# Routed attention and SoLU block: the exponentials' buffers as parts of one tile, with ScalarE's waits on itself declared away

## The chip, the cores and the metric

The kernel runs on one core of one Trainium2 chip. The time is device microseconds of one execution, from the core's first to its last work with the start and end around it; lower is better. Engines are named as in the profile: PE is TensorE (PEld its weight loads), ACT is ScalarE, DVE is VectorE, POOL is GpSimd, SP is SyncE, which here issues most DMAs. A q behind an engine (ACTq, SPq) means its sequencer, the part that waits for semaphores and issues.

## The reference

Two parts follow one another. The attention part takes q, k and v of 4 batches, 8 heads, 768 positions, 64 columns. Each query and key is assigned to the nearest of 16 normalised centroids of its head, and a query attends only to keys of its own cluster:

```python
mask = q_assign[:, :, :, None] == k_assign[:, :, None, :]
scores = scale * np.matmul(q, k.transpose(0, 1, 3, 2))
scores = np.where(mask, scores, -1000000000.0)
attn = np.exp(scores - max) ; attn = attn / (sum + 1e-09)
out = np.matmul(attn, v)
```

The heads are then laid side by side (3072 tokens of 512), and the second part computes

```python
h = x @ w_in                       # 512 -> 1024
sm = softmax(h) ; solu = h * sm
ln = (solu - mean) / sqrt(var + 1e-06) * g_ln
out = ln @ w_out                   # 1024 -> 512
```

## The kernel before

**Attention.** q and k of a pair of heads are loaded by SP into `raw` (four loads of 32 partitions for each tile, `load`, L400), turned by DVE into `xt` (L408), and cast by POOL into `qk`, whose rows below the 64 columns carry one-hot cluster rows, so that one matmul gives the score with the mask in it. `scores` (L602) fills one PSUM bank `sps` of 128 keys by up to 512 query columns; there are three such banks in rotation and 294 bank fillings in all. `expo` (L608) turns each bank into a bf16 tile `e` on ACT. There are nine `e` buffers in rotation. `values` (L625) uses 128-column pieces of `e` as matmul weights against v with a column of ones, so that numerator and denominator come out together in `ops`; `normalise` (L637, L650, DVE) divides.

**Second part.** For each of 24 blocks of 128 tokens: x is transposed (`xT`, by a DMA at L680), multiplied by w_in into two of three PSUM banks of `hreg` (`f_h`, L711), its negated maximum is taken on DVE (`f_max`, L717), ACT takes the exponential with its row sum (`f_exp`, L723, tiles `e_sb` and `esum`), DVE multiplies (`f_u`, L730), a DMA transposes `u` (L735), PE multiplies by w_out (`f_y`, L775), DVE takes the variance, POOL the factor alpha (L751 to L760, it reads `esum`), ACT or DVE scales (`f_scale`, L790, L792), and a DMA stores. The very last block is stored in two halves, and one of these halves borrows a buffer of `e_sb` as fp32.

**Order.** The two parts run interleaved. The order on each engine is written out by hand in the tables of the class `Weave`; each instruction then waits on semaphores for what it needs. Each engine counts its finished instructions in one semaphore (here named after the engine: PE, Activation and so on), and a wait is for a count.

**Buffers and waits.** Before the change, `e`, `e_sb` and `esum` are taken from pools in rotation: each use is a new tile in an old place. The framework then orders the new write behind everything that touched the old place: behind the matmuls that read it (a wait on PE) and behind the earlier write on ACT itself (a wait on Activation). An instruction of ACT holds one wait; where there are two, the program has an instruction EVENT_SEMAPHORE ahead of it that holds the other. So 275 of the 294 exponentials of L608 stand behind an EVENT_SEMAPHORE. In these the EVENT_SEMAPHORE holds the wait on PE (the later of the bank being full and the old buffer being read), and the exponential itself holds the wait on Activation. In the program the first of these waits on Activation is for count 9, ahead of the thirteenth activation of the queue that counts: the write nine exponentials back.

Of the kernel before, what the change touches and what calls it, by code (L numbers as in the profile page):

```python
# [10 lines left out]
F32 = mybir.dt.float32  # L11
BF16 = mybir.dt.bfloat16
# [3 lines left out]
Act = mybir.ActivationFunctionType  # L16
# [153 lines left out]
def kernel(  # L170
# [11 lines left out]
    nc = tc.nc  # L182
# [3 lines left out]
    P = 128  # L186
# [7 lines left out]
    d_ff = moe_w_in.shape[1]  # L194
    n_dc = d_model // P
    n_fc = d_ff // P
    FF2 = 512
    n_ff2 = d_ff // FF2
# [4 lines left out]
    exp_scale = BIAS_C / (D ** 0.5)  # L203

    const = ctx.enter_context(tc.tile_pool(name="const", bufs=1))
    big = ctx.enter_context(tc.tile_pool(name="big", bufs=1))
# [2 lines left out]
    xtp = ctx.enter_context(tc.tile_pool(name="xtp", bufs=6))  # L209
    pr = ctx.enter_context(tc.tile_pool(name="pr", bufs=3))  # L210
    vp = ctx.enter_context(tc.tile_pool(name="vp", bufs=3))
    ep = ctx.enter_context(tc.tile_pool(name="ep", bufs=9))
    mo = ctx.enter_context(tc.tile_pool(name="mo", bufs=2))
    sm = ctx.enter_context(tc.tile_pool(name="sm", bufs=4))
    ps_s = ctx.enter_context(tc.tile_pool(name="ps_s", bufs=3, space=bass.MemoryType.PSUM))
    ps_h = ctx.enter_context(tc.tile_pool(name="ps_h", bufs=1, space=bass.MemoryType.PSUM))
# [15 lines left out]
    def uses(ins, *banks, keep=90):  # L232

        for other, theirs in bank_uses[-keep:]:
            if other.ins.engine == ins.ins.engine:
                continue
            if not set(banks) & set(theirs):
                tc.declare_no_dep(ins.ins, other.ins, reason="other banks of the region")
            else:
                tc.add_manual_dep(ins.ins, other.ins.name, SYNC, reason="same bank of the region")  # L240
        bank_uses.append((ins, banks))
# [40 lines left out]
    for b in range(B):  # L282
        for p in range(n_pair):
            a, c = 2 * p, 2 * p + 1
# [38 lines left out]
    def wide(n, j):  # L323
        return sum(w for _, _, _, w, _ in UNITS[n]["banks"][j])
# [31 lines left out]
    def apart(b, p):  # L356


        return by_token(b) and not halves_of(b, p)
# [231 lines left out]


    es, sps_, opss, xs = {}, {}, {}, {}

    def scores(n, k):
        u = UNITS[n]
        b = u["b"]
        sps_[n, k] = ps_s.tile([P, 512], F32, name="sps", tag="sps")
        for h, kt, s0, w, c0 in u["banks"][k]:
            r = used(b, h)  # L600
            keys = slice(kt * P, (kt + 1) * P) if by_token(b) else slice(kt, S, n_t)
            nc.tensor.matmul(sps_[n, k][:, c0:c0 + w], side(b, h // 2, 1, h % 2, keys)[r],  # L602
                             side(b, h // 2, 0, h % 2, slice(s0 * P, s0 * P + w))[r])

    def expo(n, k):
        w = wide(n, k)
        es[n, k] = ep.tile([P, 512], BF16, name="e")
        nc.scalar.activation(es[n, k][:, :w], sps_[n, k][:, :w], Act.Exp, scale=exp_scale,  # L608
                             bias=-exp_scale)

    def place_of(n, j):

# [40 lines left out]
    xTs, ff = {}, {}  # L653
    n_f = B * n_t
# [6 lines left out]
    def pair_of(f):  # L661
        return hreg[:, 0:2, :] if f % 2 == 0 else hreg[:, 1:3, :]

    def both(f):
        return (0, 1) if f % 2 == 0 else (1, 2)
# [52 lines left out]
                                     negate=True), *both(f))  # L718

    def f_exp(f):  # L720
        ff[f, "esum"] = sm.tile([P, 1], F32, name="esum")
        ff[f, "e"] = mo.tile([P, n_ff2, FF2], BF16, name="e_sb")
        uses(nc.scalar.activation(ff[f, "e"][:], pair_of(f), Act.Exp, bias=ff[f, "nmax"][:],  # L723
                                  accum_out=ff[f, "esum"][:]), *both(f))

    def f_u(f, half=None):
        if not half:
# [20 lines left out]
    def f_eps(f):  # L748

        ff[f, "es1"] = sm.tile([P, 1], F32, name="es1")  # L750
        nc.gpsimd.tensor_scalar(ff[f, "es1"][:], ff[f, "esum"][:], scalar1=1e-3, scalar2=None,  # L751
                                op0=Alu.mult)

    def f_alpha(f):
# [25 lines left out]
    def f_scale(f, e, half=None):  # L780

        if half:
            y = mo.tile([P, n_ff2, FF2], BF16, name="e_sb")[:].rearrange(
                "p a f -> p (a f)").bitcast(F32)
        else:
            y = mo.tile([P, d_model], F32, name="y")[:]
        n = d_model if half is None else d_model // 2
        ff[f, "o", half], src = y[:, :n], (ff[f, "y"] if half is None else hreg[:, half, :n])
        if e == "ACT":
            ins = nc.scalar.activation(y[:, :n], src, Act.Copy, scale=ff[f, "alpha"][:])  # L790
        else:
            ins = nc.vector.tensor_scalar(y[:, :n], src, scalar1=ff[f, "alpha"][:], scalar2=None,  # L792
                                          op0=Alu.mult)
        if f == n_f - 1:
            uses(ins, half)
# [40 lines left out]
    for hh in range(2):  # L836
        for x in range(2):
# [19 lines left out]
                            scalar1=c_inv[:], scalar2=None, op0=Alu.mult)  # L857
# [43 lines left out]
    for idx, (b, p) in enumerate(pairs):  # L901
        first = first_of(b, p)
        if by_token(b):
            for hf, i in ((hf, i) for hf in range(2) for i in range(2)):
# [9 lines left out]
                e = "ACT" if (b, p) == (0, 0) and i == hf else "DVE"  # L914
# [5 lines left out]
        for i in range(2):  # L920
# [31 lines left out]
            for hh in range(2):  # L952
                for hf in range(2) if halves_of(b, p) else (None,):
# [3 lines left out]
                    e = "ACT" if hf is not None and i == 1 else "POOL"  # L957
# [18 lines left out]
    for idx, (b, p) in enumerate(pairs):  # L976
        first = first_of(b, p)
        for hf in range(2) if halves_of(b, p) else (None,):
# [23 lines left out]
            for j, (i, part) in enumerate(hots):  # L1002
                e = ("DVE", "POOL")[j % 2] if half else "POOL" if apart(b, p) else "SP"
# [9 lines left out]
                    (lambda e, b=b, p=p, hf=hf: blank(b, p, hf, e)),  # L1013
                    [f"pl{t}.1.{part}" for part in range(2)], also={"DVE": 0.2})

    ring_s, ring_e = 3, 9
    for i, (n, k) in enumerate(BANKS):
        u = UNITS[n]
        b = u["b"]
        p = u["subs"][0][0] // 2  # L1020
        t0 = time_of[n, k]
        nd = set()
        for h, kt, s0, w, _ in u["banks"][k]:
            p, hh = h // 2, h % 2
# [17 lines left out]
        if i >= ring_e:  # L1042
            n0, k0 = BANKS[i - ring_e]
            nd += [f"V{n0}.{j}" for j, (h, su) in enumerate(UNITS[n0]["subs"])
                   if any(spots[n0, h, su, kt][0] == k0 for kt in range(n_t))]
        add(f"E{n}.{k}", "ACT", 0.05 + wide(n, k) / 1200, t0 - 1,
            (lambda e, n=n, k=k: expo(n, k)), nd, ["E{}.{}".format(*BANKS[i - 1])] if i else [])
    prev = None
    for g, ns in enumerate(GROUPS):
# [50 lines left out]
    for f in range(n_f):  # L1100
# [15 lines left out]
        for f2 in range(n_ff2):  # L1116
            for part in range(2):
# [16 lines left out]
        nd = ([f"hm{f}"] + ([f"u{f - 2}"] if f >= 2 else []) +  # L1134
              ([f"at{f - 4}"] if f >= 4 else []))
        add(f"ex{f}", "ACT", 1.09, s + 1, (lambda e, f=f: f_exp(f)), nd)
        nd = [f"ex{f}"]
        if f >= 3:
# [16 lines left out]
        for f2 in range(n_ff2):  # L1155
# [3 lines left out]
        add(f"ag{f}", "DVE", 0.13, s + 8, (lambda e, f=f: f_aggr(f)),  # L1159
            [f"bn{f}.0", f"bn{f}.1"] + reader("al", f))  # L1160
        add(f"at{f}", "POOL", 0.22, s + 6, (lambda e, f=f: f_eps(f)), [f"ex{f}"] + reader("al", f))
        add(f"al{f}", "POOL", 1.0, s + 8, (lambda e, f=f: f_alpha(f)),
            [f"ag{f}", f"at{f}"] + reader("sc", f))
# [16 lines left out]
        if f == n_f - 1:  # L1180
            add(f"sc{f}.0", "DVE", 0.45, s + 5, (lambda e, f=f: f_scale(f, e, 0)),
                [f"y{f}.1", f"al{f}", f"ou{f - 2}"], also={"ACT": 0.36})
            add(f"ou{f}", "SP", 0.54, s + 8, (lambda e, f=f: f_out(f, 0)), [f"sc{f}.0"],
                move=0.8)
            add(f"sc{f}.1", "ACT", 0.36, s + 5, (lambda e, f=f: f_scale(f, e, 1)),
                [f"y{f}.3", f"al{f}", f"u{f}.1"], also={"DVE": 0.45})
            add(f"oz{f}", "ACT", 0.5, s + 8, (lambda e, f=f: f_out(f, 1, nc.scalar)),
                [f"sc{f}.1"])
        else:
            add(f"sc{f}", "ACT", 0.6, s + 5, (lambda e, f=f: f_scale(f, e)), nd,  # L1190
                give=None if f == n_f - 3 else "m", also={"DVE": 0.69})
            add(f"ou{f}", "SP", 0.54, s + 8, (lambda e, f=f: f_out(f)), [f"sc{f}"], move=0.8)
# [68 lines left out]
```

## Time and profile before

| | |
|---|---|
| median of three runs | 224.8 us (224.51 to 225.04) |
| span of the profiled execution | 223.1 us |
| what the median has beyond that span | 1.7 us |
| PE busy | 214.7 us, 96% of the span |
| ACT busy | 192.1 us, 86% |
| DVE busy | 197.0 us, 88% |
| exponentials of L608 | 294 instructions, 151.1 us |
| EVENT_SEMAPHORE of ACT at L608 | 275 instructions, 17 ns each |

The profile lists no whole time of the profiled execution other than its span; the span leaves out start and end. Busy time of PE is modelled and its matmuls overlap, so 96% does not mean that PE is at its peak. EVENT_SEMAPHORE is not counted as busy time. "Idle before, releaser" is the time that an engine stood still just ahead of a group of instructions, and what ended it. The chain is the work that ended last, followed back from the end.

### The profile page before, as it was taken

How to read it: one execution, taken by the hardware profiler on the slowest of the kernel's cores; microseconds unless marked ns; L12 is line 12 of the kernel's file. 1: busy time of each engine (PE TensorE's matmuls, PEld its weight loads, DVE VectorE, ACT ScalarE, POOL GpSimd, SP SyncE). 2: the span in 40 equal slices, each digit the busy share in tenths (PEclk: the TensorE clock that was granted, in tenths of full speed). 3: DMA queues.
4: the chain of work that ended last, by engine and by line, in shares of the span. 5: the costliest groups of instructions: out<-in, count | busy, mean ns of one | idle time of the engine just before them, and what ended most of it. 6: DMA issues, size and time to landing. Idle time of an engine off the chain costs nothing.

```text
span 223.1 us, 6642 instructions
## 1 busy us (share of the span) xinstructions
PE 214.7 (96%) x2422; PEld 149.8 (67%) x2454; DVE 197.0 (88%) x359; ACT 192.1 (86%) x372; POOL 127.0 (57%) x247
## 2 busy tenths in 40 slices
PE   7899999999999999999999999999999999999994
PEld 6576656677566777776577667787677777755452
DVE  3799898999999989999998999887999889888982
ACT  3779999999888999998889899999999998983363
POOL 3499842774793999547668543944796403022331
PEclk9999999999999999999999999999999999999999
DMA  6999888989999998899999879199940528385923
GB/s 151 333 299 183 240 171 240 341 203 200 166 180 180 207 156 152 190 174 205 149 268 152 175 147 240 67 207 220 223 59 9 98 51 140 79 156 148 177 80 141
DMA packets 125679, 38.80 MB, mean 174 GB/s; under 512 B 115016, under 2 KB 121168, under 8 KB 125648
## 3 DMA queue, kind: packets, MB, share of 16 engines
q1 hardware_dynamic: 123904, 37.87, 82.3%
q10 hardware_dynamic: 1744, 0.52, 1.0%
q8 instruction: 19, 0.31, 0.6%
q14 instruction: 12, 0.10, 0.1%
HBM read 23.11 MB, written 6.29 MB: 132 GB/s over the span
## 4 chain that ended last, share of the span: by engine, by line
PE 83%; ACT 5%; DVE 4%; issue 3%; DMA 3%; SPq 1%; ACTq 0%; DVEq 0%
PE sps L602 27%; PE hreg L711 17%; PE yps L775 17%; PE ops L625 14%; ACT e L608 5%; PE csc L451 4%; DMA raw<-in_q_dram 2%; PE hreg L387 1%; DVE u L730 1%; DMA raw<-in_k_dram 1%; PE hreg L575 1%; PE hreg L775 1%; PE csc L446 1%; DVE bs L741 1%; DVE xt L408 0%
## 5 line engine op out<-in xcount | busy, mean ns | idle before, releaser
L608 ACT ACTIVATE e<-sps 128x512 bf16<-128x512 f32 (+1 forms) x294 | 151.1, 599 | 12.2 <-PE sps L602 10.2
L602 PE MATMUL sps<-qk 80*128 80x256 bf16 (+5 forms) x636 | 94.0, 264 | 1.4 <-ACT e L608 0.5
L602 PEld LDWEIGHTS <-qk 80*128 80x128 bf16 (+1 forms) x636 | 60.1, 121 | 27.6 <-issue 9.0
L625 PEld LDWEIGHTS <-e 128*128 128x128 bf16 x1152 | 50.4, 97 | 12.4 <-issue 1.9
L625 PE MATMUL ops<-v,e 128*128 128x65 bf16 x1152 | 55.0, 193 | 0.1
L711 PE MATMUL hreg<-w_in_sb,xT 128*128 128x512 bf16 x173 | 49.1, 379 | 1.3 <-DVE u L730 0.2
L775 PE MATMUL yps<-w_out_c,uT 128*128 128x512 bf16 x171 | 46.5, 379 | 0.6
L515 POOL COPY qk<-oht 32x384 f32<-32x384 f32 (+1 forms) x50 | 24.4, 487 | 15.8 <-DVE oht L495 13.2
L730 DVE TENSOR_TENSOR u<-e_sb,hreg 128x1024 bf16<-128x1024 bf16 (+1 forms) x25 | 29.1, 1168 | 4.7 <-ACT e_sb L723 4.5
L741 DVE BATCH_NORM_STATS2 bs<-u 128x6 f32<-128x512 bf16 x48 | 31.5, 677 | 0.1
L717 DVE TENSOR_REDUCE nmax<-hreg 128x1 f32<-128x1024 f32 x24 | 29.0, 1209 | 2.6 <-PE hreg L711 2.2
L723 ACT ACTIVATE e_sb<-hreg,nmax 128x1024 bf16<-128x1024 f32 x24 | 26.9, 1120 | 4.5 <-DVE nmax L717 4.4
L434 POOL CAST qk<-xt 64x768 bf16<-64x768 f32 (+1 forms) x31 | 26.0, 840 | 5.0 <-DVE xt L394 3.5
L775 PEld LDWEIGHTS <-uT 128*128 128x128 bf16 x200 | 18.2, 97 | 11.7 <-issue 0.3
L757 POOL TENSOR_SCALAR esq<-es,mv 128x1 f32<-128x1 f32 x24 | 8.5, 355 | 29.4 <-DVE mv L745 21.2
L436 POOL TENSOR_SCALAR qk<-xt 64x768 bf16<-64x768 f32 (+1 forms) x28 | 22.9, 820 | 1.7
L408 DVE STREAM_TRANSPOSE xt<-raw 128x768 f32<-128x768 f32 x24 | 22.8, 955 | 0.7 <-issue 0.5
L711 PEld LDWEIGHTS <-xT 128*128 128x128 bf16 x192 | 16.7, 97 | 9.8 <-DVE u L730 1.0
L751 POOL TENSOR_SCALAR es<-esum 128x1 f32<-128x1 f32 x24 | 5.3, 221 | 26.4 <-ACT e_sb L723 25.9
L650 DVE TENSOR_TENSOR x<-ops,den 128x256 bf16<-128x256 f32 (+1 forms) x39 | 19.0, 486 | 1.3
L760 POOL TENSOR_TENSOR alpha<-esq,halves 128x1 f32<-128x1 f32 x24 | 13.5, 561 | 2.0
L533 POOL CAST v<-vf 128x384 bf16<-128x384 f32 x27 | 13.6, 516 | 1.1 <-DMA vf<-in_v_dram 0.4
(80 smaller groups left out, 167.8 us busy)
## 6 DMA issues: line engine op xcount, KB each, us to landing
vf<-in_v_dram SPq DMA_DIRECT2D x16, 384.0 KB, 4.2
out_dram<-y SPq DMA_DIRECT2D x23, 256.0 KB, 2.6
raw<-in_q_dram SPq DMA_DIRECT2D x50, 96.0 KB, 3.4
raw<-in_k_dram SPq DMA_DIRECT2D x50, 96.0 KB, 3.0
w_g<-in_moe_w_out_dram SPq DMA_DIRECT2D x4, 512.0 KB, 5.8
w_st<-in_moe_w_in_dram SPq DMA_DIRECT2D x4, 512.0 KB, 5.2
raw<-in_q_dram SPq DMA_DIRECT2D x3, 384.0 KB, 6.6
raw<-in_k_dram SPq DMA_DIRECT2D x3, 384.0 KB, 7.2
```

Source lines behind the costliest of these rows:

```text
L434: VEC[e].tensor_copy(dst, src)
L436: VEC[e].tensor_scalar(dst, src, scalar1=inv_C, scalar2=1.0, op0=Alu.mult, op1=Alu.mult)
L515: ins = VEC[e].tensor_copy(dst.bitcast(F32), src.bitcast(F32).unsqueeze(1) .to_broadcast([NB, 2, n // 2]))
L602: nc.tensor.matmul(sps_[n, k][:, c0:c0 + w], side(b, h // 2, 1, h % 2, keys)[r], side(b, h // 2, 0, h % 2, slice(s0 * P, s0 * P + w))[r])
L608: nc.scalar.activation(es[n, k][:, :w], sps_[n, k][:, :w], Act.Exp, scale=exp_scale, bias=-exp_scale)
L625: nc.tensor.matmul(opss[g][:, s, :VW], es[n, k][:, c0:c0 + P], v1[slot(b, h // 2)][:, h % 2, kt, :VW], start=(kt == 0), stop=(kt == n_t - 1))
L711: uses(nc.tensor.matmul(hreg[:, at(f, f2)[1], :], xTs[f][:, dc, :], w_in_sb[:, dc, f2 * FF2:(f2 + 1) * FF2], start=(dc == 0), stop=(dc == ...
L717: uses(nc.vector.tensor_reduce(ff[f, "nmax"][:], pair_of(f), axis=AXY, op=Alu.max, negate=True), *both(f))
L723: uses(nc.scalar.activation(ff[f, "e"][:], pair_of(f), Act.Exp, bias=ff[f, "nmax"][:], accum_out=ff[f, "esum"][:]), *both(f))
L730: uses(nc.vector.tensor_tensor(ff[f, "u"][:, at_], ff[f, "e"][:, at_], pair_of(f)[:, at_], op=Alu.mult), *banks)
L741: nc.vector.bn_stats(ff[f, "bs"][:, f2, :], ff[f, "u"][:, f2, :])
L775: ins = nc.tensor.matmul(dst, ff[f, "uT"][:, at(f, f2)[0] * (n_fc // 2) + c, :], w_out_c[:, fc, cols], start=(fc == chunks[0]), stop=(fc = ...
```

## The change

All nine `e` buffers become parts of one tile `e_ring` of 128 x 9 x 512, and the two `e_sb` buffers and the four `esum` columns become parts of `e_two` and `esums`. Each new exponential is declared independent of every earlier exponential of its kind on ACT but the last one. The waits on the matmuls that read the old contents stay.

```diff
+    e_two = big.tile([P, 2, d_ff], BF16, name="e_sb")
+    esums = big.tile([P, 4], F32, name="esum")
...
+    ring_e = 9
+    e_ring = big.tile([P, ring_e, 512], BF16, name="e")
+    e_writes, row_writes = [], []
+
+    def between(ins, writes):
+
+        for other in writes[:-1]:
+            tc.declare_no_dep(ins.ins, other.ins, query=mybir.DependencyQuery.ANY_SYNC,
+                              reason="other engines read it and are waited for in between")
+        writes.append(ins)
...
     def expo(n, k):
         w = wide(n, k)
-        es[n, k] = ep.tile([P, 512], BF16, name="e")
-        nc.scalar.activation(es[n, k][:, :w], sps_[n, k][:, :w], Act.Exp, scale=exp_scale,
-                             bias=-exp_scale)
+        es[n, k] = e_ring[:, len(e_writes) % ring_e, :]
+        ins = nc.scalar.activation(es[n, k][:, :w], sps_[n, k][:, :w], Act.Exp, scale=exp_scale,
+                                   bias=-exp_scale)
+        between(ins, e_writes)
...
     def f_exp(f):
-        ff[f, "esum"] = sm.tile([P, 1], F32, name="esum")
-        ff[f, "e"] = mo.tile([P, n_ff2, FF2], BF16, name="e_sb")
-        uses(nc.scalar.activation(ff[f, "e"][:], pair_of(f), Act.Exp, bias=ff[f, "nmax"][:],
-                                  accum_out=ff[f, "esum"][:]), *both(f))
+        ff[f, "esum"] = esums[:, f % 4:f % 4 + 1]
+        ff[f, "e"] = e_two[:, f % 2].rearrange("p (a f) -> p a f", a=n_ff2)
+        ins = nc.scalar.activation(ff[f, "e"], pair_of(f), Act.Exp, bias=ff[f, "nmax"][:],
+                                   accum_out=ff[f, "esum"])
+        uses(ins, *both(f))
+        between(ins, row_writes)
...
         if half:
-            y = mo.tile([P, n_ff2, FF2], BF16, name="e_sb")[:].rearrange(
-                "p a f -> p (a f)").bitcast(F32)
+            y = e_two[:, n_f % 2].bitcast(F32)
```

On ACT's queue before, from the first exponentials on (names as in the program; the brackets give the semaphores that an instruction and the EVENT_SEMAPHORE ahead of it wait for, x counts equal neighbours):

```order
L608 ACTIVATE e<-sps 128x384 [waits PE_49] x9
L608 ACTIVATE e<-sps 128x384 [waits PE_49,Activation_49] x3
L394 COPY xt<-hreg 128x384 [waits DVE_49,PE_49] x2
L608 ACTIVATE e<-sps 128x384 [waits Activation_49]
L608 ACTIVATE e<-sps 128x384 [waits PE_49,Activation_49] x2
L608 ACTIVATE e<-sps 128x384 [waits PE_49] x3
L394 COPY xt<-hreg 128x384 [waits DVE_49,Pool_49]
L608 ACTIVATE e<-sps 128x384 [waits PE_49] x2
L608 ACTIVATE e<-sps 128x384 [waits PE_49,Activation_49]
L608 ACTIVATE e<-sps 128x384 [waits PE_49] x3
L608 ACTIVATE e<-sps 128x512 [waits PE_49,Activation_49] x52
L723 ACTIVATE e_sb,esum<-hreg,nmax 128x1024 [waits DVE_49]
```

The same stretch after, where lines are some 11 further down:

```order
L619 ACTIVATE e<-sps 128x384 [waits PE_49] x12
L395 COPY xt<-hreg 128x384 [waits DVE_49,PE_49] x2
L619 ACTIVATE e<-sps 128x384 [waits PE_49] x6
L395 COPY xt<-hreg 128x384 [waits DVE_49,Pool_49]
L619 ACTIVATE e<-sps 128x384 [waits PE_49] x6
L619 ACTIVATE e<-sps 128x512 [waits PE_49] x52
L735 ACTIVATE e_sb,esum<-hreg,nmax 128x1024 [waits DVE_49]
```

No instruction moved; the Activation waits are gone from all exponentials. Counted over ACT's queue, 306 EVENT_SEMAPHOREs become 32. Five of the scalings at L790 get an Activation wait that an exponential ahead of them used to carry, and in two of them that is one EVENT_SEMAPHORE more. On PE, DVE, POOL and SP every instruction and every wait, with its count, is what it was.

The places of the tiles in SBUF move with the pools. Three that matter below, by byte address within a partition:

| tile | before | after |
|---|---|---|
| `raw`, first of eight | 118144 (a multiple of 128) | 131488 (32 past a multiple of 128) |
| `vf`, first of three | 170656 (32 past a multiple of 64) | 184000 (a multiple of 64) |
| `e`, first of nine | 179872 | 105888 |

More of the change, by code (lines that the diff above doesn't have):

```diff
@@ L211 @@
     vp = ctx.enter_context(tc.tile_pool(name="vp", bufs=3))
-    ep = ctx.enter_context(tc.tile_pool(name="ep", bufs=9))
     mo = ctx.enter_context(tc.tile_pool(name="mo", bufs=2))
+    e_two = big.tile([P, 2, d_ff], BF16, name="e_sb")
+    esums = big.tile([P, 4], F32, name="esum")
     sm = ctx.enter_context(tc.tile_pool(name="sm", bufs=4))
@@ L750, in f_eps @@
         ff[f, "es1"] = sm.tile([P, 1], F32, name="es1")
-        nc.gpsimd.tensor_scalar(ff[f, "es1"][:], ff[f, "esum"][:], scalar1=1e-3, scalar2=None,
+        nc.gpsimd.tensor_scalar(ff[f, "es1"][:], ff[f, "esum"], scalar1=1e-3, scalar2=None,
                                 op0=Alu.mult)
@@ L1014 @@
                     [f"pl{t}.1.{part}" for part in range(2)], also={"DVE": 0.2})
-    ring_s, ring_e = 3, 9
+    ring_s = 3
     for i, (n, k) in enumerate(BANKS):
```

## The prediction

> **What bounds the kernel now.** I read the busy table and the slices first, then the chain, then the exponentials' line with its waits. The page's tables:
>
> ```profile
> span 223.1 us, 6642 instructions
> PE 214.7 (96%) x2422; PEld 149.8 (67%) x2454; DVE 197.0 (88%) x359; ACT 192.1 (86%) x372; POOL 127.0 (57%) x247
> PE   7899999999999999999999999999999999999994
> ACT  3779999999888999998889899999999998983363
> DMA  6999888989999998899999879199940528385923
> PE 83%; ACT 5%; DVE 4%; issue 3%; DMA 3%; SPq 1%; ACTq 0%; DVEq 0%
> ```
>
> PE is full from the first microseconds to the end, the DMA engines are nearly full for three fifths of the span, and the chain that ended last runs 83% over PE and 5% (some 11 us) over ACT. So PE's work is the bound, and ACT can give back only what PE waits for it. The same by stages (columns: length, then busy us and instructions of PE, PEld, DVE, ACT, POOL, then clock, DMA share, GB/s):
>
> ```profile
> 20.00:60.00 40.00, 38.67 (x496) 26.77 (x495) 36.41 (x69) 38.44 (x78) 25.16 (x43) 1.00 0.96 218
> 60.00:140.00 80.00, 79.20 (x903) 56.17 (x918) 76.40 (x129) 73.52 (x141) 53.45 (x97) 1.00 1.02 184
> ```
>
> From 20 to 60 us ACT is as full as PE (38.4 and 38.7 of 40 us); later PE leads. The granted clock is 1.00, so it plays no part.
>
> **What the change removes.** The row of L608 has the instruction that goes:
>
> ```profile
> L608 ACT ACTIVATE e<-sps x294: 485/597/712, 9.9 to 200.5; 128x512 bf16<-128x512 f32 x135, 128x384 bf16<-128x384 f32 x12
> L608 ACTq EVENT_SEMAPHORE  x275: 17/17/17, 14.3 to 199.9; - x138
> ```
>
> The wait on Activation is for a write nine exponentials back, over 4 us ago at 0.5 us each; it never ends last, so its removal is worth nothing by itself. What it costs is the form: PE's count is waited for in the separate instruction. How long that takes is read from the chain in pieces (start, length, what):
>
> ```profile
> 15.64 0.34 PE hreg L387 x3
> 15.98 0.02 issue
> 16.00 0.02 ACT xt L394
> ...
> 25.06 0.34 PE sps L602 x2
> 25.40 0.02 issue
> 25.42 0.02 ACTq L608
> 25.43 0.04 issue
> 25.48 0.18 ACT e L608
> ...
> 32.83 0.02 ACTq L608
> ...
> 37.90 0.02 ACTq L608
> ...
> 41.52 0.02 ACTq L608
> 41.54 0.10 issue
> ```
>
> At 25.40 PE's matmul ends, and the exponential starts at 25.48: 0.02 of signal, 0.02 of EVENT_SEMAPHORE, 0.04 until the start, 0.08 us. At 15.98 a copy that holds PE's wait itself starts 0.02 us after the matmul. So each exponential that ACT stands ready for starts 0.06 us sooner; where ACT is still busy with the one before, the EVENT_SEMAPHORE lies under it and costs nothing. (At 41.52 the start comes 0.12 after the EVENT_SEMAPHORE began; I count 0.06 there too.) [...]
>
> How many pay? The waits, longest first:
>
> ```profile
> ACT e L608 <- PE sps L602: 10.2, 27, 1.0
> PEld L602 <- ACT e L608: 1.5, 3, 0.6
> PE sps L602 <- ACT e L608: 0.5, 2, 0.3
> ```
>
> Columns: us in all, times, longest. 27 exponentials have ACT idle long enough ahead of them to be listed. Upper end: all 275 times 0.06 is 16.5 us, which the page excludes (ACT's whole idle time ahead of them is 10.2 us); all 27 in series give 27 x 0.06 = 1.6 us. Lower end: only those on the chain, the four at 25.42, 32.83, 37.90 and 41.52, and their gain lost again, 0. In between: a gain reaches the end where PE then waits for ACT. The chain shows four such places, the two rows of PE and PEld have five waits for exponentials (3 and 2; some may be the ends of those four, while `e_sb`, which stands behind exponentials in ACT's queue, is left out). I take nine: 9 x 0.06 = 0.54 us. That lies near the lower end because PE has the long row in the chain, not ACT.
>
> **The smaller parts.** That the change might not do what it says is excluded by the two programs: 306 EVENT_SEMAPHOREs on ACT become 32. 274 instructions fewer to fetch: nothing that a row shows. The row maximum's exponential (L723) loses one Activation wait in 24: nothing, it waits for DVE. Two scalings (L790) get one EVENT_SEMAPHORE more: at most 2 x 0.06 = 0.12 us if both stand ready, and 0 where POOL's alpha or PE's product, which they wait for too, comes later than that. `e` and `e_sb` in new places: exponentials and weight loads of equal shape but other places all take what their shape takes, as these show:
>
> ```profile
> L625 PEld LDWEIGHTS <-e 128*128 128x128 bf16 x1152 | 50.4, 97 | 12.4 <-issue 1.9
> L775 PEld LDWEIGHTS <-uT 128*128 128x128 bf16 x200 | 18.2, 97 | 11.7 <-issue 0.3
> ```
>
> 97 ns for both tiles; I cost the place of `e` at nothing. The place of `raw` is a rival below.
>
> **Sum.** 0.54 us off the span of 223.1, so 222.6; the runs' median of 224.8 lies 1.7 above that span, and with the same 1.7 it becomes 224.3 us, 0.2% less. About 0.2% (0.45 us) is what a measurement of this kernel can tell from no change, so the forecast stands just beyond that line.
>
> **Rival one: the gain is hidden, 224.7 us.** Whatever ACT gains from 20 to 55 us may end here:
>
> ```profile
> 55.29 2.11 DMA raw<-in_k_dram
> 57.40 0.49 issue
> 57.89 0.98 DVE xt L408
> ```
>
> The chain goes through a load of k, whose issue waits in SP's queue behind transposes and earlier loads, not for an exponential. Then the four places before 55 us count nothing, and from 60 us on the same list of waits has only this row of PE or PEld for an exponential:
>
> ```profile
> PEld L602 <- ACT e L608: 0.6, 1, 0.6
> ```
>
> So one place, 0.06 us, or two if one too short to be listed goes with it: about 0.1 us. For it: DMA is at 0.96 of its time in that stage. Against it: only this one place of the chain has a load on it after the start, and DVE's u, itself behind ACT, stands just ahead.
>
> **Rival two, the other side: the loads get slower, 225.6 us.** The new pools put `raw` 32 bytes past a multiple of 128. These are the queue (packets, MB, share of 16 engines' span) and the loads (KB each, us to landing):
>
> ```profile
> q1 hardware_dynamic: 123904, 37.87, 82.3%
> raw<-in_q_dram SPq DMA_DIRECT2D x50, 96.0 KB, 3.4
> raw<-in_k_dram SPq DMA_DIRECT2D x50, 96.0 KB, 3.0
> vf<-in_v_dram SPq DMA_DIRECT2D x16, 384.0 KB, 4.2
> raw<-in_q_dram SPq DMA_DIRECT2D x3, 384.0 KB, 6.6
> ```
>
> 96 of these 100 loads are of 32 floats (128 bytes) at a time, 768 pieces each: 73,728 pieces, over half of the queue's packets, on 16 engines whose packets take 0.823 x 223.1 x 16 / 123904 = 24 ns on the average. Each nanosecond more per piece is 73,728 / 16 = 4.6 us of the DMA engines, about 1.25 us of it (27%) by 57.9 us, where the load landed 0.49 us ahead of its reader. So it decides from about 0.8 ns per piece, which would take up both that slack and the 0.54 us; no row gives the price, and I take 6% of the average packet, 1.4 ns: 1.4 x 1.25 - 0.49 = 1.3 us later there, less the gain 0.8, so 225.6. For it: the pieces no longer start on multiples of their own size, and DMA is full until 140 us. Against it: of the last two rows, which move equal amounts, `vf` lay 32 past a multiple of 64 and `raw` on one, and `vf` landed sooner; `vf` now moves onto a multiple of 64, so what one loses the other may win. [...]
>
> **Chances.** The gain as summed or more: 0.45 (224.3, from 223.4 if most of the 27 waits count to 224.35). Hidden, or too small to tell: 0.36 (224.35 to 225.25). Loads slower: 0.19 (beyond 225.25). The likeliest is the first, 224.3; its own range is 223.4 to 224.4. The range for 8 in 10 reaches from 223.4, where 23 of the 27 waits would pay (23 x 0.06 = 1.4), to 225.6, the price of the second rival.
>
> **What would show it.** In the changed kernel's profile the row EVENT_SEMAPHORE of the exponential's line is gone or nearly, and in the chain PE's end and the exponential's start are 0.02 apart. The median duration of an exponential stays 597 ns. If the sum is right, the idle time "ACT e <- PE sps" gets longer or stays (ACT is done sooner, and waits for PE more), and PE's waits on ACT e shrink below the 2.0 us of the two rows. If rival one holds, the chain still has the 2 us load near 57 us at the same time as before. If rival two holds, the share of queue q1 rises above 82.3% and the loads' landing above 3.0 and 3.4 us. Wrong would be the forecast if exponentials start no sooner after PE with the wait in the instruction itself, or if a load is late where none was.

## The result and the profile after

| | before | after |
|---|---|---|
| median | 225.14 us (22 runs, 224.45 to 227.15) | 228.16 us (22 runs, 225.57 to 232.14) |
| ratio | | 1.0074, 95% interval 1.0046 to 1.0102 |
| span of the profiled execution | 223.1 us | 224.6 us (its time 226.53 us) |

The change makes the kernel slower. The ratio leaves out executions over 1.5% above a kernel's fastest, of which the changed kernel has many, so it stands below the ratio of the medians, which is 228.16 / 225.14 = 1.013.

The page of the changed kernel, the lines that answer to those shown of before (span, DMA by slices, the chain, the exponentials):

```profile
span 224.6 us, 6368 instructions
DMA  7999999999999999999999999688950629266923
PE 78%; DMA 8%; DVE 6%; ACT 2%; SPq 2%; issue 2%; POOL 0%; DVEq 0%
...
L619 ACT ACTIVATE e<-sps x294: 485/597/712, 10.0 to 202.1; 128x512 bf16<-128x512 f32 x135, 128x384 bf16<-128x384 f32 x12
```

The chain now runs 78% over PE (83% before), 2% over ACT (5% before) and 8% over DMA (3% before). On the chain, DMA has taken the place of ACT. The stretches (columns as before):

```profile
20.00:60.00 40.00, 38.23 (x490) 26.23 (x490) 35.05 (x67) 37.27 (x75) 23.74 (x40) 1.00 1.08 214
60.00:140.00 80.00, 79.20 (x891) 55.91 (x907) 76.19 (x128) 73.71 (x141) 54.58 (x98) 1.00 1.22 180
```

The DMA engines were at 0.96 and 1.02 of their time and are now at 1.08 and 1.22, while the data rate did not rise (218 and 184 GB/s before, 214 and 180 now): the same bytes take longer. (The share adds up the times of all packets; at 1.08 and 1.22 of the 16 engines' time, packets overlap.) The queue and the loads show which (share of 16 engines; us to landing last):

```profile
q1 hardware_dynamic: 123904, 37.87, 92.9%
...
vf<-in_v_dram SPq DMA_DIRECT2D x16, 384.0 KB, 4.5
...
raw<-in_q_dram SPq DMA_DIRECT2D x50, 96.0 KB, 4.0
raw<-in_k_dram SPq DMA_DIRECT2D x50, 96.0 KB, 3.8
```

The number of packets and the bytes are what they were. The share goes from 82.3% to 92.9%, and the loads of `raw` land after 4.0 and 3.8 us where it was 3.4 and 3.0. In engine time that is 0.929 x 224.6 - 0.823 x 223.1 = 25 us on each of 16 engines. The trace lists every packet. Those of 128 bytes are 73,728 in number, just the pieces of `raw` that the prediction counted; their mean goes from 13.5 to 16.8 ns, so 73,728 x 3.3 ns / 16 = 15 of the 25 us are theirs. The pieces of 256 bytes go from 26.2 to 29.3 ns; most of them, 34,304, are those of the DMA transposes, which go through the queue q1 as the loads do and go from 26.9 to 30.3 ns, another 34,304 x 3.4 ns / 16 = 7 us.

Where it hurts is in the waits and in the chain of the changed kernel:

```profile
ACT e L619 <- PE sps L613: 10.5, 24, 1.2
...
PEld L723 <- DMA xT<-x: 2.0, 3, 1.1
PEld L613 <- ACT e L619: 1.5, 3, 0.6
...
PE hreg L723 <- DMA xT<-x: 0.8, 1, 0.8
...
PEld hreg L576 <- DMA w_g<-in_moe_w_out_dram: 0.6, 1, 0.6
...
PE sps L613 <- ACT e L619: 0.5, 2, 0.3
```

```profile
22.82 5.96 DMA raw<-in_k_dram
...
40.63 6.76 DMA xT<-x
...
55.78 0.43 PE hreg L723 x2
56.21 0.44 PE sps L613 x4
...
81.08 0.25 PE sps L613 x2
81.33 0.02 issue
81.35 0.61 ACT e L619
...
116.66 4.33 DMA raw<-in_q_dram
```

Three rows are new. PE's weight loads wait 0.6 us for `w_g`, a load of weights (`w_out`) that took 7.2 us from its issue at 30.1 to landing, where it took 5.9 before. And PE waits 0.8 us, its weight loads 2.0 us, for `xT`, the transposed x (the 0.8 us lie within the longest of the weight loads' waits). Its DMA at 40.63 is 6.76 us on the chain, in flight beside loads of weights, k and q; the same transpose took 5.5 us before. PE's waits for exponentials are what they were, 1.5 and 0.5 us. And one thing came as foretold: at 81.33 PE ends and 0.02 us later the exponential starts. The row EVENT_SEMAPHORE of the exponentials' line is gone.

### The profile page after: what moved, and what is told of

It is laid out like the page before. It is cut to its first block, busy times and chain, and to the rows that moved or that the text cites. A ratio compares the mean times of both kernels' runs of the same rounds, so it can differ in the third digit from the quotient of the medians.

```text
span 224.6 us, 6368 instructions
## 1 busy us (share of the span) xinstructions
PE 216.6 (96%) x2422; PEld 150.9 (67%) x2454; DVE 196.9 (88%) x359; ACT 192.8 (86%) x372; POOL 127.4 (57%) x247
## 3 DMA queue, kind: packets, MB, share of 16 engines
q1 hardware_dynamic: 123904, 37.87, 92.9%
## 4 chain that ended last, share of the span: by engine, by line
PE 78%; DMA 8%; DVE 6%; ACT 2%; SPq 2%; issue 2%; POOL 0%; DVEq 0%
PE sps L613 23%; PE yps L789 16%; PE hreg L723 16%; PE ops L637 13%; PE csc L452 3%; DMA xT<-x 3%; DMA raw<-in_k_dram 3%; PE hreg L388 2%; DMA raw<-in_q_dram 2%; ACT e L619 2%; PE idle_p L833 2%; SPq L401 1%; DVE cst L461 1%; PE hreg L576 1%; PE hreg L789 1%
## 5 line engine op out<-in xcount | busy, mean ns | idle before, releaser
L619 ACT ACTIVATE e<-sps 128x512 bf16<-128x512 f32 (+1 forms) x294 | 151.3, 600 | 12.8 <-PE sps L613 10.5
L735 ACT ACTIVATE e_sb<-hreg,nmax 128x1024 bf16<-128x1024 f32 x24 | 26.9, 1120 | 4.5 <-DVE nmax L729 4.3
L774 POOL TENSOR_TENSOR alpha<-esq,halves 128x1 f32<-128x1 f32 x24 | 13.5, 563 | 2.0
```

Of the source, the lines that this page charges most:

```text
L619: ins = nc.scalar.activation(es[n, k][:, :w], sps_[n, k][:, :w], Act.Exp, scale=exp_scale, bias=-exp_scale)
L735: ins = nc.scalar.activation(ff[f, "e"], pair_of(f), Act.Exp, bias=ff[f, "nmax"][:], accum_out=ff[f, "esum"])
```

## The experiments

Theory A: the loads are slower because `raw` no longer starts at a multiple of 128 bytes; the waits that were taken away are worth little. Theory B: the lost time comes from the waits, since ACT now works in another rhythm and collides with loads it used to miss. Theory C: some other tile that moved (`e`, `vf`, `xT`, `uT`) is at fault. The expectations call them P, W and O. All kernels compute the whole result. Ratios are to the kernel before, run beside each on the same chip.

Why `raw` moved at all: `e_two` (4096 bytes), `esums` (16 bytes in a place of 32) and `e_ring` (9216 bytes) now stand in the pool `big`, ahead of `raw`. They are 13344 bytes, 104 times 128 and 32 more. So the tile of 16 bytes shifts every tile behind it off its multiple of 128.

### Only `raw` moved, in the kernel before

```diff
     wst = ctx.enter_context(tc.tile_pool(name="wst", bufs=4))
+    gap = ctx.enter_context(tc.tile_pool(name="gap", bufs=1)).tile([P, 8], F32, name="gap")
     ld = ctx.enter_context(tc.tile_pool(name="ld", bufs=8))
+    gap2 = ctx.enter_context(tc.tile_pool(name="gap2", bufs=1)).tile([P, 24], F32, name="gap2")
```

`ld` is the pool of `raw`. 32 unused bytes go ahead of it and 96 behind, so that `raw` stands 32 past a multiple of 128 and all tiles behind it move by 128. In a second kernel both are 64 bytes.

> The kernel before with 32 unused bytes ahead of raw and 96 behind it: only raw is moved to 32 past a multiple of 128, every other tile keeps its remainder of 128. Theory P: q1 about 91 to 93%, ratio 1.006 to 1.012. Theory W: 1.000. Theory O (the place of another tile, xt, w_st, vf, xT or uT, does it): 1.000 here, and 1.007 or more in the kernel where all of them move.

> As the kernel with only raw moved, but by 64 bytes: each piece of 128 bytes starts on a multiple of 64, not of 128. If a piece's cost goes by blocks of 64 bytes: as before, ratio 1.000, q1 82%. If by blocks of 128 or 256 bytes: as slow as with 32, ratio 1.006 to 1.012, q1 above 90%. Theory W: 1.000.

Measured: 1.0111 (1.0054 to 1.0168) with 32 bytes, 1.0128 (1.0089 to 1.0167) with 64. The page of the first:

```profile
q1 hardware_dynamic: 123904, 37.87, 90.1%
...
raw<-in_k_dram SPq DMA_DIRECT2D x50, 96.0 KB, 3.7
```

Its waits:

```profile
PEld L713 <- DMA xT<-x: 4.7, 3, 2.4
PE hreg L713 <- DMA xT<-x: 3.5, 2, 2.1
PEld L604 <- ACT e L610: 1.5, 3, 0.6
```

The page of the second:

```profile
q1 hardware_dynamic: 123904, 37.87, 89.4%
...
raw<-in_k_dram SPq DMA_DIRECT2D x50, 96.0 KB, 3.9
```

With nothing of the change but the place of `raw`, the queue's share and the landing of k come near those of the changed kernel, and the time goes up as there. That is theory A. The instruction that reads `raw`, the STREAM_TRANSPOSE, takes 955 ns in the kernel before and in the changed one, so it is not the reader that got slower. 32 and 64 bytes cannot be told apart. The two pages are of long executions, of 231.04 and 232.13 us, so their waits are larger than those of a median one. And a wait for `xT` or `w_g` in one execution is no sign of the place of `raw`: further down, a long execution with `raw` well placed has both (1.7 and 0.7 us, of 226.95), and one with `raw` badly placed has neither (226.23). The share of q1 and the landing of k do go with the place.

### More moved, or all but `raw`

```diff
     big = ctx.enter_context(tc.tile_pool(name="big", bufs=1))
+    gap = ctx.enter_context(tc.tile_pool(name="gap", bufs=1)).tile([P, 8], F32, name="gap")
     wst = ctx.enter_context(tc.tile_pool(name="wst", bufs=4))
```

In the kernel before, everything from the staging of weights on moves by 32 bytes.

> The kernel before with one unused tile of 32 bytes ahead of the pools, so that raw, xt and w_st lie 32 past a multiple of 128 and vf, xT and uT on a multiple of 64, as in the changed kernel; all waits as before. Theory P: as slow as the changed kernel or slower, ratio 1.007 to 1.012, q1 about 93%, landing 3.8 to 4.0 us. Theory W: ratio 1.000, q1 82%.

Measured: 1.023 (1.0179 to 1.0282), q1 at 90.6%. `raw` is off its multiple and the time goes up, but by more than with `raw` alone and more than expected. What the rest adds here is not settled: the next kernel moves the same tiles but `raw` and the staging of weights, without cost, and the staging was not moved alone.

```diff
     ld = ctx.enter_context(tc.tile_pool(name="ld", bufs=8))
+    gap = ctx.enter_context(tc.tile_pool(name="gap", bufs=1)).tile([P, 8], F32, name="gap")
```

The 32 bytes behind `raw`: `xt`, `vf`, `e`, `xT`, `uT` and the rest move to where they stand, counted from a multiple of 128, in the kernel above; `raw` and the staging of weights stay.

> The kernel before with 32 unused bytes behind raw: raw stays on a multiple of 128, and xt, vf, e, x, xT, u, uT, y move by 32, to where they stand against multiples of 64 and 128 in the changed kernel. Theory P: ratio 1.000, q1 82 to 84%. Theory O (the others' places add to it; the kernel with all moved was slower than the one with raw moved, 1.023 against 1.011): about 1.01.

Measured: 1.0002 (0.9967 to 1.0036), q1 at 83.0%. And with the tiles from `vf` on put on multiples of 128 (they stood 32 past one):

```diff
     pr = ctx.enter_context(tc.tile_pool(name="pr", bufs=3))
+    gap = ctx.enter_context(tc.tile_pool(name="gap", bufs=1)).tile([P, 24], F32, name="gap")
```

> The kernel before with 96 unused bytes behind the tiles of the cluster assignment: vf, e, x, xT, e_sb, u, uT, y move from 32 past a multiple of 128 onto one, raw stays on one. If the transposes' pieces of 256 bytes pay for their place too: ratio 0.995 to 0.999 and the landing of uT and xT below 3.7 and 3.1 us. If only the loads of raw pay: 1.000.

Measured: 0.9996 (0.9967 to 1.0025). Its page:

```profile
q1 hardware_dynamic: 123904, 37.87, 79.4%
```

The share falls by 2.9 points, and `uT` and `xT` land after 3.6 and 2.7 us where it was 3.7 and 3.1, so these tiles' places count for the DMA engines too, but the time does not answer. Theory C falls: the tiles behind `raw` can move either way without a change in time that could be told.

### The change, with `raw` back on a multiple of 128

```diff
-    esums = big.tile([P, 4], F32, name="esum")
+    esums = big.tile([P, 32], F32, name="esum")
```

The changed kernel with its waits still away; only this tile grows from 16 to 128 bytes, of which 16 are used.

> The changed kernel with the four row sums in a tile of 128 bytes instead of 16, so that every tile behind it moves by 96 bytes: raw is on a multiple of 128 again, and vf, xT and uT are 32 past one, as before the change. The waits stay declared away. Theory P (the loads' pieces of 128 bytes take longer because raw lies 32 bytes past a multiple of 128): queue q1 back to 82 to 83%, landing of the raw loads 3.0 to 3.4 us, ratio to before 0.996 to 1.000. Theory W (the missing waits themselves make it slower, for instance by starting exponentials at moments that hurt PE): ratio stays near 1.007, q1 may be anything.

Measured: 224.47 us, 0.9957 (0.9926 to 0.9989). Its page:

```profile
q1 hardware_dynamic: 123904, 37.87, 83.0%
...
raw<-in_q_dram SPq DMA_DIRECT2D x50, 96.0 KB, 3.8
raw<-in_k_dram SPq DMA_DIRECT2D x50, 96.0 KB, 3.0
```

One number turns the change from a loss into no loss. Theory B falls with it, for the waits are away here as well. The share of q1 and the landing of k are back as expected; the landing of q is not (3.8 us, in one of the longest executions), so it says little on the place. Then with `raw` where it was before counted from a multiple of 256 (128 past it), while in the kernel above it is on one:

```diff
-    esums = big.tile([P, 4], F32, name="esum")
+    esums = big.tile([P, 64], F32, name="esum")
```

> The changed kernel with a sums' tile of 256 bytes: raw 128 bytes past a multiple of 256, where it was in the kernel before; with the tile of 128 bytes it was on a multiple of 256. If multiples of 128 are what counts, it gives what the tile of 128 bytes gave, 0.993 to 0.999, with q1 at 82 to 84%. If it is multiples of 256, it differs from that tile's kernel by some half per cent or more, and q1 by some points.

Measured: 0.9982 (0.9944 to 1.0019), q1 at 83.5%. On a multiple of 256 or 128 past one is the same within the measurement. So of the four places tried, a multiple of 256 and 128 past one are good, and 32 and 64 past a multiple of 128 are bad.

Next, the changed kernel with every tile at its old address (the parts of one tile are taken from pools in the old order, with four sums in four places of 32 bytes):

```diff
...
-    esums = big.tile([P, 4], F32, name="esum")
...
-    e_ring = big.tile([P, ring_e, 512], BF16, name="e")
+    e_ring = ep.tile([P, ring_e, 512], BF16, name="e")
...
+            e_rows["sum"] = sm.tile([P, 4, 8], F32, name="esum", bufs=1)
+            e_rows["e"] = mo.tile([P, 2, d_ff], BF16, name="e_sb", bufs=1)
```

> The changed kernel's waits (32 instead of 306 EVENT_SEMAPHOREs on ACT) with every tile of SBUF at the address it had before the change: the ring of e and the two buffers of e_sb are allocated in the pools and in the order of before. So only the waits differ. Theory P (the place of raw alone made the change slower, the waits are a gain): ratio 0.994 to 0.998, 0.54 us by the prediction's sum and 1.0 us by the run with the row sums in 128 bytes. Theory W (the missing waits cost): above 1.000. If the gain of that run came from other tiles' new places, 1.000 here.

Measured: 0.9993 (0.9959 to 1.0028), q1 at 82.3%. The loss is gone, but the gain of 0.2 to 0.6% that was expected does not show. And with the tiles from `vf` on, too, on multiples of 128, which compares with the kernel before that had them there:

```diff
+    gap = ctx.enter_context(tc.tile_pool(name="gap", bufs=1)).tile([P, 24], F32, name="gap")
...
-    esums = big.tile([P, 4], F32, name="esum")
+    esums = big.tile([P, 32], F32, name="esum")
```

> The changed kernel's waits, the row sums in 128 bytes, and 96 unused bytes as in the run beside it, so that every large tile lies on a multiple of 128. If places of raw and transposes both count: faster than the kernel with the row sums in 128 bytes alone, ratio 0.990 to 0.995. If only raw's: the same as that one, 0.994 to 0.997.

Measured: 0.9981 (0.9952 to 1.0011), less of a gain than either range expected. Its page and its waits:

```profile
q1 hardware_dynamic: 123904, 37.87, 79.3%
...
PE 85%; ACT 6%; DVE 4%; DMA 2%; issue 1%; SPq 0%; DVEq 0%
```

```profile
ACT e L620 <- PE sps L614: 8.6, 21, 0.8
PEld L614 <- ACT e L620: 1.5, 3, 0.6
```

The kernel before with the same tiles on multiples of 128 has this:

```profile
ACT e L609 <- PE sps L603: 9.7, 26, 0.8
PEld L603 <- ACT e L609: 1.5, 3, 0.6
```

These two traces are the clean pair for what the waits are worth, as neither loses time to loads (the table of starts further down has no step up in either). ACT stands 1.1 us less ahead of its exponentials, with five places fewer; 21 places times 0.06 us would be 1.3.

### The waits back, at the bad and at the good place

```diff
-        between(ins, e_writes)
+        e_writes.append(ins)
...
-        between(ins, row_writes)
+        row_writes.append(ins)
```

The changed kernel with its addresses but without the declarations; then the same with the tile of 128 bytes; beside them the changed kernel again.

> The changed kernel once more, beside the three below that differ from it by one edit each. Both theories expect what was measured before: 1.005 to 1.010 of the kernel before, q1 busy some 93%, raw landing after 3.8 to 4.0 us.

> The changed kernel with the same places but with ScalarE's waits on its own earlier writes left in (an EVENT_SEMAPHORE ahead of each exponential, as before). If the place of raw and the waits add up, the waits cost what they cost at the good place (0 to 0.4%): 1.008 to 1.014 of the kernel before. If the loads now set the time so much that the wait is hidden behind them, it is the changed kernel's own 1.005 to 1.010. If the lost time had been due to the waits that were taken away (an order of ScalarE that suits TensorE less), the kernel comes back to 0.998 to 1.003. The starts of the exponentials go back to 0.08 us after TensorE's end, and q1 stays above 90%.

> As the one above (waits left in), with the sums' tile of 128 bytes instead of 16, so that raw stands on a multiple of 128 again: the buffers are parts of one tile, and nothing else of the change is left. The theory of raw's place expects 0.998 to 1.002 of the kernel before and q1 near 83%. If parts of one tile cost by themselves (other waits between ScalarE, TensorE and VectorE), it is slower than 1.003.

Measured, in one table with the kernels above:

| | waits left in | waits away |
|---|---|---|
| `raw` 32 past a multiple of 128 | 1.0088 (1.0046 to 1.0129) | 1.0102 (1.0061 to 1.0142), first 1.0074 (1.0046 to 1.0102) |
| `raw` on a multiple of 128 | 0.9976 (0.9947 to 1.0006) | 0.9957 (0.9926 to 0.9989), 0.9982 (0.9944 to 1.0019) |

Down a column the time changes by 0.9 to 1.5%, along a row by nothing that can be told. The 1.0088 lies in two of the ranges that were expected, waits that add up and waits that are hidden, and does not choose between them. That the waits are really back shows the line in the first of the two:

```profile
L619 ACTq EVENT_SEMAPHORE  x276: 17/17/17, 14.3 to 201.2; - x138
```

Its queue still is slow, if below the 90% that were expected:

```profile
q1 hardware_dynamic: 123904, 37.87, 88.8%
```

And the second, with the waits in and `raw` on a multiple of 128:

```profile
q1 hardware_dynamic: 123904, 37.87, 82.4%
```

### Where the time goes within a run

From the traces: by how many us an exponential starts later (+) or sooner (-) than the same one in the trace of before. Each column is one execution.

```
exponential, start   after  after   waits in  sums 128  all 128,   before,   before,
before, us                  again   raw +32   raw +0    waits away all 128   raw +32
  0     9.88         +0.09  -0.21    0.00     +0.12     +0.12      +0.37     -0.02
 28    24.21         +0.03  -0.27    0.00     -0.14     +0.07      +0.38     -0.01
 56    39.41         +0.79  +1.89   +0.26     +0.94     -0.04      +0.37     +0.55
 84    54.87         +1.63  +3.12   +0.26     +2.36     -0.17      +0.38     +2.11
140    93.05         +1.44  +2.96   +1.30     +2.06     -0.53      +0.01     +2.11
168   113.22         +1.62  +3.24   +1.31     +2.04     -0.56      +0.02     +6.06
293   200.53         +1.55  +3.16   +1.28     +1.99     -0.62      +0.03     +6.07
```

All of the loss arises between 24 and 113 us, in the stretches where the DMA engines are at 0.96 to 1.22 of their time; from 113 us on nothing changes any more. How much is lost differs from one execution to the next: the execution of "sums 128" shown here took 226.95 us, the longest of its twelve, whose median is 224.47. The two columns "all 128" differ by 0.25 us at the first exponential, where no wait had been removed yet, and by 0.65 at the last: 0.40 us is what the waits are worth in this pair. It comes mostly in steps of 0.05 to 0.06 us, which stay from then on, at the exponentials 30, 41, 59, 65 and 205, with smaller ones by 24 and 86; the 0.07 of exponential 9 is lost again by the 12th. It is one execution of each kernel, and the medians of their twelve (225.24 and 224.98 us) do not show it.

## Why the prediction was wrong

The forecast was 224.3 us, and the likeliest case was not the one that came: 228.16 us, outside the range, on the side of rival two. By the ratio, 1.0074 x 225.14 = 226.8 us, it lies outside too.

- **The step that failed is the price of the place of `raw`: the sum put it at nothing, and rival two at "no row gives the price, and I take 6% of the average packet, 1.4 ns".** It is 3.3 ns per piece of `raw` on the average in this trace, and 1.8 to 3.8 in those of the other kernels with `raw` badly placed. Put into the prediction's own sum, 3.3 x 1.25 - 0.49 less the gain of 0.54 gives 3.1 us and so 227.9 us; the medians differ by 3.0. That this comes so near is in part luck, as the sum puts all of the loss at one load where the traces do not have it. The cause that rival two names, the place of `raw`, its count of 73,728 pieces and both signs (the share of q1 and the landings above their old values) were right. With the point at 0.8 ns "from which it decides" so low, and a price unknown from below nothing upwards, the chance of 0.19 was too small, and the range should have gone on to what a quarter more per piece (3.3 of 13.5 ns) does.
- **The reason against it did not hold.** It was that `vf` landed sooner than `raw` though it stood worse, and that `vf` now moves onto a multiple of 64. The kernel that moves all but `raw`, `vf` onto a multiple of 64 among it, is at 1.0002: `vf` gives nothing back. It lands after 4.2 us there, as before. Nor do the two rows compared tell a price: both are of pieces of 1536 bytes, and the loads of q in that row land after 6.3 us in the changed kernel where it was 6.6, though `raw` stands worse. The 73,728 pieces are those of the other rows.
- **That the place of `raw` counts** had no price from a row in the prediction; the runs gave one. With `raw` 32 and 64 bytes past a multiple of 128 in the kernel before, the time is 1.0111 and 1.0128 of what it was; with `raw` on a multiple of 256 in the changed kernel it is 0.9957, and 128 past one it is 0.9982. In the kernel before, half of the pieces start on a multiple of 256 and half 128 past one, and 97.6% of all take at most 16 ns, so between these two starts no price shows. Which pieces are the slow ones no trace shows.
- **The place of that loss** was put at the load at 55.29 us. The traces put it elsewhere and at several places. In that of the changed kernel the exponentials fall 0.78 us behind at 38 us, where PE's weight loads wait for `w_g`, and 0.87 us more at 47 us, where PE waits for the transpose `xT`. Neither is a load of `raw`. At 55 us its chain runs over PE, and the load of q at 116.66, though on the chain, costs nothing against before.
- **0.06 us per exponential** was right. In the trace of before, the exponentials that ACT stands ready for (over 0.15 us idle) start 83 ns after PE's signal in the median of 28; in the changed kernel all 25 start 22 or 23 ns after it. Where ACT has no pause, an exponential of 512 columns starts 477 ns after the one before in the median of both traces (181 and 177 pairs), so there the EVENT_SEMAPHORE costs nothing.
- **"Nine places"** was six or seven: 0.40 us in the clean pair of executions, where 0.54 was forecast. They were looked for in the wrong rows. PE's waits on ACT were to shrink below 2.0 us; they stay at 1.5 and 0.5 in the changed kernel. And "ACT e <- PE sps" was to get longer or stay; it is 10.5 us where it was 10.2, but in the clean pair it is the shorter, since the idle time ahead of an exponential holds the 0.06 us too. The five full steps that stay have a pause of ACT of 0.14 to 0.16 us in the trace of before, which shrinks to 0.08 to 0.11; a wait is listed from 0.15 us on, so they stand at the lower edge of the list or just below it.
- **Rival one** is right in part. In the trace of the kernel with sums of 256 bytes the exponentials gain 0.18 us on the kernel before, counted from the first one, by 31 us and are 1.0 us behind it at 39 us, after PE's weight loads have waited 1.0 us for `w_g`: the gain is swallowed. Over all runs with `raw` in a good place, waits away and waits in cannot be told apart (0.9957 to 0.9993 against 0.9976 to 1.0002).
- **"I cost the place of `e` at nothing"** was right: the median of an exponential is 597 ns in both, and the kernels with `e` 0, 32 and 64 past a multiple of 128 are at 0.9957 to 1.0002 whenever `raw` is well placed. That parts of one tile cost nothing by themselves is shown by the kernel with only them (0.9976, 0.9947 to 1.0006).

## What to carry to other kernels

A tile added to a pool moves every tile behind it, here `raw` and `vf` by 13344 bytes. Compare the addresses that small DMA pieces are written to before any thought on waits: here, for pieces of 128 bytes and multiples of 128, 16 bytes of sums cost 1%, and 112 unused bytes behind them took it back. DMA was as busy here as the engine that bounds the kernel (between 20 and 140 us of the kernel before, 0.96 and 1.02 of its time against 0.97 and 0.99 for PE), and the loss came out as waits for other transfers (weights, a transpose), at places that differ from one execution to the next, so look at the queue's share and the times of its packets rather than at the load's own readers. A wait held by an EVENT_SEMAPHORE ahead of the exponential starts it 0.06 us later where ACT stands ready (83 ns after PE's signal against 22 or 23); in the clean pair that reached the later exponentials mainly where ACT had a pause of 0.14 to 0.16 us, and it did not show in the medians.

## What the runs showed of the hardware

- Not every piece gets slower. With `raw` on a multiple of 128, 97.6% of the 128-byte packets in the trace of before take at most 16 ns, nearly all 11 or 13. In the changed kernel 72.9% do, 10% take 17 to 22 ns and 17% take longer, 31 ns in their mean. With 32 and 64 bytes of shift in the kernel before, 76% and 78% take at most 16 ns. So a quarter of the pieces takes up to twice and more, and the rest what it took. Why a quarter is open.
- How much slower varies within a run and between executions. In stretches of 10 us between 20 and 140 us the share of 128-byte packets over 16 ns runs from 9% (100 to 110 us) to 61% (80 to 90 us) in the changed kernel's trace. Its runs spread over 6.6 us, those of before over 2.7.
- The kernel with all tiles from the staging of weights on shifted by 32 bytes lost twice as much as the one with `raw` alone (1.023 against 1.0111) at the same share of q1 (90.6% and 90.1%). The medians of all their executions, 231.69 and 230.03 us, stand closer, and each has only six. This is open.
- In the trace of before, 337 of ACT's 338 ACTIVATEs hold one wait and one holds none; the 275 EVENT_SEMAPHOREs at L608 hold the second waits of their exponentials, and 345 of ACT's instructions raise its semaphore.
